# A scheduling planner whose costs for the time before the second mixture of experts become finer

## The chip, the cores and the metric

The kernel runs on one core of a Trainium2 chip. The metric is the device time of one execution in microseconds; the median of three runs before the change is 1993.34 us (1993.1 to 1995.27).

## The reference

Attention over 4 batches and 8 heads (576 tokens, head size 64) with a causal mask and a bias from a running sum, then a dense two-layer network with a gated activation, then a mixture of eight experts whose weights come out of eight rounds of row and column balancing:

```python
def _attn_ref(q, k, v, s):
    scores = np.matmul(q, k.transpose(0, 1, 3, 2)) / np.sqrt(D)
    cum = np.cumsum(np.maximum(s, 0.0), axis=-1)
    bias = -(cum[:, :, :, None] - cum[:, :, None, :])
    scores = np.where(causal, -1e9, scores + np.minimum(bias, 0.0))
    ...
    return np.matmul(attn, v)

def _moe_ref(x, w_in, w_out):          # 2304 x 512, hidden size 2048
    h = x @ w_in
    g = h * (1.0 / (1.0 + np.exp(-1.702 * h)))
    return g @ w_out

def _moe2_ref(x, w_gate, w1, w2):      # 8 experts, hidden size 1024
    P = balanced(np.exp(x @ w_gate))   # eight rounds
    for e in range(E):
        out += P[:, e:e + 1] * (np.maximum(x @ w1[e], 0.0) @ w2[e])
```

## The kernel before, in words

The program has three stages that overlap. **Attention** runs over 64 heads (each of the 32 is taken in two parts, 256 and 320 query rows). TensorE computes scores (`sp`), VectorE adds the mask and finds the extreme (`sm`, the ISA rows), ScalarE takes the exponential, TensorE turns the result (`tp`), it is copied to `pf` (early heads, one copy) or to `ph` and `pl` (later heads, two halves in 16 bits), TensorE multiplies by v (`op`), and VectorE finishes the head: a sum, a reciprocal, and the product `xg`. There is one bank for `op`, so the next head's `op` begins only when `xg` of the last is done. Finished rows are turned (`xtp`) into `xh` and `xl`.

**The first mixture** (in the code `moe`, it is one dense network) goes over nine blocks of 256 tokens and eight pairs of hidden slices. `hp` is the first product and `acc` the second; between them stand `t` (ScalarE's tanh, a VectorE product), `gh` (a cast) and `gl` (the rest). Its weights come as 64-bit words and have to be converted first: 32 chunks, each with two ScalarE passes over `st`, a VectorE operation `t<-st`, a cast to `wih` or `woh`, and a difference to `wil` or `wol`. Seven blocks are interleaved with attention; the last two run together, as `accw`, at its end. **The second mixture** (experts) follows; its operations are `A` to `D`, `h`, `y`.

What runs when is decided by a planner, the class `Sequencer`, while the program is built. Every operation is handed to `submit`, which asks `cost` for its duration; operations of TensorE are issued at once, those of the other engines are held and issued in the order in which the model says they can start (`run`, `issue`, `depend`). TensorE's next unit of work is chosen in the main loop: of six kinds (value products, turns, scores, first mixture last) the first whose inputs the model has ready at TensorE's modelled time. So the costs set the order of instructions on all engines, and nothing else about the program. They also set which engine takes a copy or a difference:

```python
    def any_copy(out, in_):
        if seq.load("DVE") <= seq.load("ACT"):
            nc.vector.tensor_copy(out, in_)
        else:
            nc.scalar.copy(out=out, in_=in_)

    def any_less(out, a, b, bias=POOL_BIAS):
        engine = nc.vector if seq.fine or seq.load("DVE") + bias <= seq.load("POOL") else nc.gpsimd
        engine.tensor_tensor(out=out, in0=a, in1=b, op=ALU.subtract)
```

The flag `fine` is set in `begin_second`, ahead of `accw`; from there on the finer costs were in use before the change too.

Of the kernel before, what the change touches and what calls it, by code (L numbers as in the profile page):

```python
# [10 lines left out]
F32R = mybir.dt.float32r  # L11
# [22 lines left out]
BYTES = {F32: 4, F32R: 4, I32: 4, F16: 2, BF16: 2, U8: 1}  # L34
# [4 lines left out]
N_KF = 4  # L39
ADDING = 3.6  # L40
AFTER_OWN = 34
N_F = 14
NEXT_V = 11
LATE = 3000.0
# [5 lines left out]


class Op:
    __slots__ = ("engine", "call", "cost", "ready", "end", "waits", "after", "rank", "number", "nbytes", "late", "tail")


class Sequencer:
# [10 lines left out]
    def __init__(self):  # L67
        self.free = dict.fromkeys(self.ENGINES, 0.0)
        self.held = {e: [] for e in self.ENGINES}
        self.touched = {}  # L70
        self.earlier = {}
        self.rings = {}
        self.dma = self.issued = 0.0
        self.rank = 0
        self.holding = False
        self.fine = False
        self.late = 0.0
        self.count = 0
        self.outside = set()
# [50 lines left out]
    def cost(self, engine, what, out, ins, sums=False):  # L130
        n = max(self.size(x) for x in [out] + ins[:2])
        psum = any(x.space == PSUM for x in ins)
        if self.fine:
            if engine == "PE":
                return self.size(out) * (4 if ins[0].dtype == F32 else 1) / 2.4 + (13 if ins[0].dtype == F32R else 2.7)
            by = any(self.size(x) == 1 for x in ins[1:]) and n > 1
            if engine == "DVE":
                quick = what in ("tensor_copy", "tensor_scalar") and not psum
                return 66 + 60 * by + n / (1.92 if quick else 0.96)
            if engine == "ACT":  # L140
                return (50 if psum else 90) + 100 * by + 93 * sums + n / 1.2
        if engine == "PE":
            n = self.size(out)
            if what == "transpose":
                return 2 * n / 2.4
            slow = ins[0].dtype == F32 or ins[0].dtype == F32R and n < 256
            return n * (4 if slow else 1) / 2.4
        if engine == "DVE":
            quick = what in ("tensor_copy", "tensor_scalar") and not psum
            return 70 + n / (1.92 if quick else 0.96)  # L150
        if engine == "ACT":
            return 90 + n / 1.2
        return 80 + n * {"memset": 0.3, "tensor_scalar": 2.7}.get(what, 2.24)


    def submit(self, engine, what, call, outs, ins, adds=False):
        op = Op()
        op.engine, op.call, op.end, op.rank, op.number = engine, call, None, self.rank, self.count
        op.ready, op.waits, op.after, op.nbytes, op.tail = 0.0, set(), [], 0, 0
        op.late = self.late + (2000 if self.fine and self.rank else 0)  # L160
        self.count += 1
        if what == "dma_start":
            op.cost = 60 if engine == "SP" else 1000
            op.nbytes = self.size(outs[0]) * outs[0].shape[0] * (2 if self.fine and outs[0].dtype == F16 else 4)
            if adds and self.fine:
                op.nbytes *= ADDING
        else:
            sums = len(outs) > 1
            op.cost = self.cost(engine, what, outs[0], ins, sums) + (190 if sums and not self.fine else 0)
            if self.fine:  # L170
                op.tail = {"DVE": 85, "ACT": 110}.get(engine, 0) + 90 * sums
        for ap, writes in [(x, False) for x in ins] + [(x, True) for x in outs]:
            name = ap.tensor.name
            if name in self.outside:
# [19 lines left out]
    def depend(self, op, on):  # L194
        if on.end is None:
            op.waits.add(on)
            on.after.append(op)
        elif self.fine and on.engine == op.engine != "PE" and not on.nbytes:
            op.ready = max(op.ready, on.end + AFTER_OWN)
        elif on.engine != "PE" or op.engine != "PE":  # L200
            op.ready = max(op.ready, on.end + LATENCY.get((on.engine, op.engine), LATENCY.get(on.engine, 0)))

    def issue(self, op):
        for x in sorted(op.waits, key=lambda x: x.number):
            if x.end is None:
                self.issue(x)
        e = op.engine
        start = max(self.free[e], op.ready)
        self.free[e] = start + op.cost
        op.end = start + op.cost + op.tail  # L210
        if op.nbytes:
            self.issued = max(self.issued, start) + 475
            self.dma = max(self.dma, self.issued + 1200) + op.nbytes / 360
            op.end = self.dma + 440 + op.late
        if op in self.held[e]:
            self.held[e].remove(op)
        op.call()
        op.call = None
        for x in op.after:
            x.waits.discard(op)  # L220
            self.depend(x, op)
        op.after = None

    def when(self, op):

# [2035 lines left out]
```

## Time and profile before

| | |
|---|---|
| median of three runs | 1993.34 us |
| the profiled execution | 1995.91 us |
| its span, first to last instruction | 1994.1 us |
| TensorE busy | 98% of the span |
| VectorE, ScalarE, GpSimd busy | 72%, 62%, 17% |
| first `hp`, first `accw` | 55.3 us, 573.67 us |

All instructions are recorded by one helper, so that they all carry its line, L279; they are told apart by the names of their tiles. The busy share of TensorE is high because its matmuls follow each other closely; gaps show in the view of who waits for whom. In that view and in the order of time, the bracket behind a row is the engine's idle time just before it and the instruction that ended it. "head 8" below is the eighth reciprocal over `stats` on VectorE.

### The profile page before, as it was taken

Reading aid. Unit: us, or ns where it says so; the run is one execution under the profiler, and the core shown is the slowest. Engines: PE = TensorE matmul, PEld = TensorE weight load, DVE = VectorE, ACT = ScalarE, POOL = GpSimd, SP = SyncE. Lnnn points to the kernel's source line nnn. Section 1 sums busy time; section 2 is a strip of 40 time slices with the busy share of each in tenths; the row PEclk is TensorE's granted clock in tenths of the full one; section 3 lists DMA queues with packets and bytes.
Section 4 is the critical chain, followed back from the end, with each engine's and each line's share of the span. In section 5 each row is a group of like instructions: output and inputs, shape, how many; then the busy total and the mean of one; then the engine's idle time right before and its main releaser. Section 6 shows DMA issues by size and latency. Waiting matters only on the chain.

```text
span 1994.1 us, 41095 instructions
## 1 busy us (share of the span) xinstructions
PE 1956.2 (98%) x15683; PEld 1575.5 (79%) x15683; DVE 1427.6 (72%) x3240; ACT 1227.5 (62%) x2525; POOL 335.0 (17%) x376
## 2 busy tenths in 40 slices
PE   6999999999999999999999999999999999999999
PEld 5889999999988677777777777777777777777777
DVE  5886776776743776887877767776787776776656
ACT  4776765766643665665666666656666666565343
POOL 3565444443300000000000011111100001111000
PEclk9999999999999999999999999999999999999999
DMA  7555444454335544565484565666648556566331
GB/s 221 159 178 181 138 131 138 129 146 116 86 94 186 208 152 146 202 232 182 147 273 133 153 186 156 172 197 184 167 120 261 147 150 186 156 172 183 119 130 43
DMA packets 230100, 322.11 MB, mean 162 GB/s; under 512 B 38272, under 2 KB 156224, under 8 KB 229904
## 3 DMA queue, kind: packets, MB, share of 16 engines
q1 hardware_dynamic: 216944, 295.90, 45.2%
q0 software_dynamic: 12960, 23.60, 8.2%
q8 instruction: 123, 2.02, 0.4%
q14 instruction: 73, 0.60, 0.1%
HBM read 230.85 MB, written 84.34 MB: 158 GB/s over the span
## 4 chain that ended last, share of the span: by engine, by line
PE 81%; DVE 9%; ACT 6%; DMA 2%; issue 1%; SPq 0%; POOL 0%; ACTq 0%; DVEq 0%
PE C L279 16%; PE A L279 16%; PE D L279 16%; PE hp L279 8%; PE B L279 8%; PE acc L279 5%; PE op L279 3%; PE sp L279 3%; PE tp L279 2%; ACT h L279 2%; PE accw L279 2%; DVE h L279 2%; DVE t L279 1%; DVE hst L279 1%; PE accx L279 1%
## 5 line engine op out<-in xcount | busy, mean ns | idle before, releaser
L279 PEld LDWEIGHTS <-h 128*128 128x128 f16 x6048 | 591.3, 98 | 86.3 <-issue 7.6
L279 PEld LDWEIGHTS <-w1o 128*128 128x128 f16 x4036 | 394.6, 98 | 255.1 <-issue 4.5
L279 POOL DMA_DIRECT2D acc_d<-y x90 | 77.8, 865 | 1186.5 <-DVE y L279 662.1
L279 PE MATMUL C<-xt,w1o 128*128 128x384 f16 x1152 | 218.6, 326 | 1.4 <-DVE hst L279 1.4
L279 PE MATMUL D<-xt,w1o 128*128 128x384 f16 x1152 | 218.4, 326 | 0.0
L279 PE MATMUL D<-w2o,h 128*128 128x256 f16 x1728 | 217.7, 273 | 0.2 <-ACT y L279 0.2
L279 PE MATMUL A<-xt,w1o 128*128 128x384 f16 x1152 | 214.8, 326 | 0.1
L279 PE MATMUL A<-w2o,h 128*128 128x256 f16 x1728 | 212.2, 273 | 1.7 <-ACT B L279 1.4
L279 PE MATMUL C<-w2o,h 128*128 128x256 f16 x1728 | 208.4, 273 | 2.5 <-DVE y L279 1.7
L279 DVE SCALAR_TENSOR_TENSOR h<-hst,h 128x768 f16<-128x768 f32 (+1 forms) x192 | 139.1, 755 | 55.9 <-ACT h L279 55.9
L279 ACT COPY C<-B 128x384 f32<-128x384 f32 (+1 forms) x168 | 71.5, 426 | 153.8 <-PE B L279 92.7
L279 PE MATMUL hp<-xh,wih 128*128 128x256 f32 (+1 forms) x512 | 154.4, 302 | 1.3 <-DVE t L279 0.7
L279 PE MATMUL hp<-xl,wih 128*128 128x256 f32 (+1 forms) x512 | 152.0, 297 | 0.0
L279 PE MATMUL hp<-xh,wil 128*128 128x256 f32 (+1 forms) x512 | 151.8, 297 | 0.0
L279 ACT ACTIVATE h<-hst 128x768 f16<-128x768 f32 (+1 forms) x192 | 126.2, 678 | 3.8 <-DVE hst L279 3.8
L279 ACT ACTIVATE sm<-sm,stats 64x576 f32<-64x576 f32 (+4 forms) x160 | 94.5, 600 | 34.0 <-DVE stats L279 33.7
L279 PE MATMUL acc<-gh,woh 128*128 128x256 f32 x384 | 110.9, 289 | 0.0
L279 PE MATMUL B<-w2o,h 128*128 128x256 f16 x864 | 110.5, 273 | 0.1
L279 PE MATMUL B<-xt,w1o 128*128 128x384 f16 x576 | 109.3, 326 | 0.0
L279 PE MATMUL acc<-gl,woh 128*128 128x256 f32 x384 | 108.5, 282 | 0.0
L279 PE MATMUL acc<-gh,wol 128*128 128x256 f32 x384 | 108.3, 282 | 0.0
L279 ACT COPY B<-A 128x384 f32<-128x384 f32 (+1 forms) x168 | 70.2, 425 | 58.4 <-PE A L279 57.6
(242 smaller groups left out, 4041.8 us busy)
## 6 DMA issues: line engine op xcount, KB each, us to landing
xt<-xc_d SPq DMA_DIRECT2D x168, 384.0 KB
wm<-in_moe_w_dram SPq DMA_DIRECT2D x112, 256.0 KB
w2o<-w_d SPq DMA_DIRECT2D x56, 512.0 KB
wr<-in_moe_w_dram SPq DMA_DIRECT2D x112, 256.0 KB
w_d<-wo SPq DMA_DIRECT2D x98, 256.0 KB
acc_d<-y POOLq DMA_DIRECT2D x90, 256.0 KB, 4.8
kq<-in_qk_dram SPq DMA_DIRECT2D x32, 448.0 KB
st<-in_moe_w_in_dram SPq DMA_DIRECT2D x16, 512.0 KB
```

The costliest lines, as they stand in the source:

```text
L279: self.seq.submit(self.name, what, lambda: method(*args, **named), outs, ins, "accum_op" in named)
```

## The change

The finer costs, until now used after `begin_second` only, are used from the start. For VectorE and ScalarE this means another base duration, 60 or 100 ns more where an operand is one number per row, no flat 190 ns for an operation with a second output, a tail of 85 or 110 ns (90 more with a second output) after which a result counts as there, and 34 ns between two operations of one engine. TensorE gets 2.7 or 13 ns per matmul, a weight load that shows where the matmul before it is shorter, and twice the time for everything until 6300 ns have passed without a gap of over 50 ns (`array`). No operation of the program is added or taken away but for the choice of engine.

```diff
--- before.py
+++ after.py
@@ -39,6 +39,7 @@
 N_KF = 4
 ADDING = 3.6
 AFTER_OWN = 34
+WARM = 6300
 N_F = 14
 NEXT_V = 11
 LATE = 3000.0
@@ -50,7 +51,7 @@
 
 
 class Op:
-    __slots__ = ("engine", "call", "cost", "ready", "end", "waits", "after", "rank", "number", "nbytes", "late", "tail")
+    __slots__ = ("engine", "call", "cost", "ready", "end", "waits", "after", "rank", "number", "nbytes", "late", "tail", "load")
 
 
 class Sequencer:
@@ -74,6 +75,7 @@
         self.rank = 0
         self.holding = False
         self.fine = False
+        self.cold, self.since, self.streamed = True, 0.0, 0.0
         self.late = 0.0
         self.count = 0
         self.outside = set()
@@ -133,30 +135,25 @@
         if self.fine:
             if engine == "PE":
                 return self.size(out) * (4 if ins[0].dtype == F32 else 1) / 2.4 + (13 if ins[0].dtype == F32R else 2.7)
-            by = any(self.size(x) == 1 for x in ins[1:]) and n > 1
-            if engine == "DVE":
-                quick = what in ("tensor_copy", "tensor_scalar") and not psum
-                return 66 + 60 * by + n / (1.92 if quick else 0.96)
-            if engine == "ACT":
-                return (50 if psum else 90) + 100 * by + 93 * sums + n / 1.2
         if engine == "PE":
             n = self.size(out)
             if what == "transpose":
-                return 2 * n / 2.4
+                return 2 * n / 2.4 + 3
             slow = ins[0].dtype == F32 or ins[0].dtype == F32R and n < 256
-            return n * (4 if slow else 1) / 2.4
+            return n * (4 if slow else 1) / 2.4 + (13 if ins[0].dtype == F32R else 2.7)
+        by = any(self.size(x) == 1 for x in ins[1:]) and n > 1
         if engine == "DVE":
             quick = what in ("tensor_copy", "tensor_scalar") and not psum
-            return 70 + n / (1.92 if quick else 0.96)
+            return 66 + 60 * by + n / (1.92 if quick else 0.96)
         if engine == "ACT":
-            return 90 + n / 1.2
+            return (50 if psum else 90) + 100 * by + 93 * sums + n / 1.2
         return 80 + n * {"memset": 0.3, "tensor_scalar": 2.7}.get(what, 2.24)
 
 
     def submit(self, engine, what, call, outs, ins, adds=False):
         op = Op()
         op.engine, op.call, op.end, op.rank, op.number = engine, call, None, self.rank, self.count
-        op.ready, op.waits, op.after, op.nbytes, op.tail = 0.0, set(), [], 0, 0
+        op.ready, op.waits, op.after, op.nbytes, op.tail, op.load = 0.0, set(), [], 0, 0, 0
         op.late = self.late + (2000 if self.fine and self.rank else 0)
         self.count += 1
         if what == "dma_start":
@@ -166,9 +163,10 @@
                 op.nbytes *= ADDING
         else:
             sums = len(outs) > 1
-            op.cost = self.cost(engine, what, outs[0], ins, sums) + (190 if sums and not self.fine else 0)
-            if self.fine:
-                op.tail = {"DVE": 85, "ACT": 110}.get(engine, 0) + 90 * sums
+            if engine == "PE":
+                op.load = 110 if BYTES[ins[0].dtype] == 4 else 27
+            op.cost = self.cost(engine, what, outs[0], ins, sums)
+            op.tail = {"DVE": 85, "ACT": 110}.get(engine, 0) + 90 * sums
         for ap, writes in [(x, False) for x in ins] + [(x, True) for x in outs]:
             name = ap.tensor.name
             if name in self.outside:
@@ -195,7 +193,7 @@
         if on.end is None:
             op.waits.add(on)
             on.after.append(op)
-        elif self.fine and on.engine == op.engine != "PE" and not on.nbytes:
+        elif on.engine == op.engine != "PE" and not on.nbytes:
             op.ready = max(op.ready, on.end + AFTER_OWN)
         elif on.engine != "PE" or op.engine != "PE":
             op.ready = max(op.ready, on.end + LATENCY.get((on.engine, op.engine), LATENCY.get(on.engine, 0)))
@@ -206,6 +204,8 @@
                 self.issue(x)
         e = op.engine
         start = max(self.free[e], op.ready)
+        if e == "PE" and not self.fine:
+            start = self.array(op, start)
         self.free[e] = start + op.cost
         op.end = start + op.cost + op.tail
         if op.nbytes:
@@ -220,6 +220,19 @@
             x.waits.discard(op)
             self.depend(x, op)
         op.after = None
+
+    def array(self, op, start):
+
+        idle = start > self.free["PE"] + 50
+        if idle:
+            self.since = start
+        if start - self.since > WARM:
+            self.cold = False
+        by = 2 if self.cold else 1
+        op.cost *= by
+        begin = start + max(0.0, by * op.load - (0.0 if idle else self.streamed))
+        self.streamed = op.cost
+        return begin
 
     def when(self, op):
 
```

From the first `accw` on, VectorE, ScalarE, GpSimd and TensorE have the same instructions in the same order as before; ahead of it, 19 operations more stand on VectorE, 22 fewer on ScalarE and 3 more on GpSimd. Two places in the order follow.

VectorE between the eighth and the ninth head, before. `sm` belongs to the ninth head's scores, `pf` to its turned results, `xl` to the first mixture's input, `st` and `t64` to the conversion of weights:

```order
L279 ISA sm_547,stats_124<-sp_562,mask_120,stats_124 64x288
L279 ISA stats_124 64x1
L279 ISA sm_569,stats_124<-sp_570,mask_120 128x384
L279 ISA stats_124 128x1
L279 COPY pf_579<-tp_574 128x512
L279 ISA sm_593,stats_124<-sp_594,mask_120 128x512
L279 ISA stats_124 128x1
L279 TENSOR_TENSOR xl_128<-xtp_582,xh_127 128x4x128
L279 CAST one0_112<-kq_360 128x896
L279 SCALAR_TENSOR_TENSOR t64_280<-st_258 128x512
L279 COPY pf_621<-tp_615 128x320
L279 TENSOR_TENSOR xl_128<-xtp_601,xh_127 128x4x128
```

The same place after the change, from the cast of the tenth head's keys (`one0`) on:

```order
L292 CAST one0_112<-kq_340 128x896
L292 ISA sm_561,stats_124<-sp_567,mask_120,stats_124 64x288
L292 ISA stats_124 64x1
L292 TENSOR_TENSOR xl_128<-xtp_546,xh_127 128x4x128
L292 CAST woh1_78<-t64_283 128x512
L292 SCALAR_TENSOR_TENSOR t64_349<-st_262 128x512
L292 COPY pf_589<-tp_585 128x384
L292 TENSOR_TENSOR xl_128<-xtp_553,xh_127 128x4x128
L292 ISA sm_593,stats_124<-sp_594,mask_120 128x384
L292 ISA stats_124 128x1
L292 TENSOR_TENSOR wol1_79<-t64_349,woh1_78 128x512
L292 COPY pf_614<-tp_609 128x512
```

The copy of the ninth head's first turned block, `pf_589`, now has a conversion `t64`, a cast `woh1` and an `xl` right ahead of it (another conversion, `t64_283`, stands just above the rows shown); before, that copy, `pf_560`, stood two rows above the rows shown. A difference, `wol1`, now stands ahead of the second copy `pf_614`.

TensorE while the fifth to eighth head end, before. `vtp` and `vbp` are two small matmuls for the scaling of v; the products `op` of the fifth head stand behind `vtp`:

```order
L279 MATMUL vtp_459<-ident_60,vmax_138 2x128
L279 MATMUL op_462<-vf0_133,pf_404 128x65 x2
L279 MATMUL op_462<-vf1_134,pf_404 128x65
L279 MATMUL tp_466<-ident_60,sm_378 128x128 x3
L279 MATMUL op_487<-vf0_133,pf_438 128x65 x2
L279 MATMUL op_487<-vf1_134,pf_438 128x65
L279 MATMUL vbp_491<-vd_412,ones_b_140 128x4
L279 MATMUL tp_493<-ident_60,sm_406 128x128 x3
L279 MATMUL op_515<-vf0_133,pf_470 128x65 x2
L279 MATMUL op_515<-vf1_134,pf_470 128x65
```

and after:

```order
L292 MATMUL op_455<-vf0_133,pf_404 128x65 x2
L292 MATMUL op_455<-vf1_134,pf_404 128x65
L292 MATMUL tp_460<-ident_60,sm_378 128x128 x3
L292 MATMUL vtp_472<-ident_60,vmax_138 2x128
L292 MATMUL op_482<-vf0_133,pf_439 128x65 x2
L292 MATMUL op_482<-vf1_134,pf_439 128x65
L292 MATMUL tp_488<-ident_60,sm_408 128x128 x3
L292 MATMUL vbp_503<-vd_414,ones_b_140 128x4
L292 MATMUL op_509<-vf0_133,pf_464 128x65 x2
L292 MATMUL op_509<-vf1_134,pf_464 128x65
```

`vtp` has moved from ahead of the fifth head's products to ahead of the sixth's; `vbp` has moved from behind the sixth head's products and ahead of a turn to behind that turn.

## Rows read from the trace of the kernel before

**Rows 1.** Busy time of TensorE over the span, from the page; us, share, instructions.

```profile
PE 1956.2 (98%) x15683; PEld 1575.5 (79%) x15683; DVE 1427.6 (72%) x3240; ACT 1227.5 (62%) x2525; POOL 335.0 (17%) x376
```

**Rows 2.** Stretches: us, then busy time of each engine (instructions), clock, DMA share, GB/s.

```profile
47.00:158.00 111.00, 103.78 (x913) 96.63 (x912) 97.13 (x254) 85.33 (x164) 65.84 (x63) 0.97 0.53 168
110.00:160.00 50.00, 44.81 (x392) 42.46 (x391) 47.47 (x109) 37.12 (x78) 34.05 (x31) 0.93 0.63 206
158.00:573.70 415.70, 411.17 (x4016) 393.76 (x4015) 293.22 (x863) 268.04 (x545) 174.53 (x191) 1.00 0.45 130
573.70:1994.00 1420.30, 1410.13 (x10643) 1059.67 (x10642) 1009.98 (x2034) 852.97 (x1776) 77.81 (x90) 1.00 0.56 168
```

**Rows 3.** The same view, two stretches in which the granted clock fell.

```profile
110.00:120.00 10.00, 7.49 (x56) 6.37 (x55) 9.59 (x28) 8.82 (x20) 5.53 (x6) 0.70 0.67 227
120.00:130.00 10.00, 10.00 (x95) 9.79 (x95) 8.97 (x20) 7.12 (x17) 6.69 (x8) 0.96 0.93 300
```

**Rows 4.** Who TensorE waited for, 8.6 to 573.6 us; total, times, longest.

```profile
PE op L279 <- DVE xg L279: 6.7, 7, 2.4
PE op L279 <- DVE pl L279: 2.6, 4, 1.1
PE vtp L279 <- DVE vmax L279: 1.8, 1, 1.8
PE op L279 <- DVE pf L279: 0.3, 1, 0.3
```

**Rows 5.** TensorE in order of time, opening; start, duration, idle before in brackets.

```profile
44.60 1.51 PE L279 MATMUL op<-vf,pf 128*128 128x65 f32 x6
48.15 1.05 PE L279 MATMUL tp<-ident,sm 128*128 128x128 f32 x4
50.64 0.60 PE L279 MATMUL xtp<-ident,xg 128*128 128x128 f32 x4
55.30 0.36 PE L279 MATMUL hp<-xh,wih 128*128 128x256 f32 x1
55.50 0.28 PE L279 MATMUL hp<-xl,wih 128*128 128x256 f32 x1
55.62 0.28 PE L279 MATMUL hp<-xh,wil 128*128 128x256 f32 x1
```

**Rows 6.** VectorE in order of time: reciprocals of the eighth, ninth and twenty-third head.

```profile
47.01 0.16 DVE L279 RECIPROCAL stats<-stats 128x2 f32<-128x2 f32 x1
55.24 0.17 DVE L279 RECIPROCAL stats<-stats 128x3 f32<-128x3 f32 x1
157.98 0.16 DVE L279 RECIPROCAL stats<-stats 128x2 f32<-128x2 f32 x1
```

**Rows 7.** VectorE groups by form, 47 to 170 us; busy, mean ns, idle before.

```profile
L279 DVE SCALAR_TENSOR_TENSOR t<-st 128x512 int32<-128x512 int32 x26 | 25.2, 974 | 1.1 <-POOL wol L279 0.7 <-ACT va L279 0.3
L279 DVE CAST woh<-t 128x512 fp32r<-128x512 f32 x10 | 7.0, 696 | 0.1
L279 DVE CAST wih<-t 128x512 fp32r<-128x512 f32 x8 | 6.2, 770 | 0.0
L279 DVE TENSOR_TENSOR wol<-t,woh 128x512 fp32r<-128x512 f32 x3 | 4.9, 1621 | 2.2 <-ACT woh L279 2.2
L279 DVE TENSOR_TENSOR one<-kq,one 64x320 fp32r<-64x320 f32 x3 | 4.3, 1420 | 0.1
L279 DVE TENSOR_TENSOR v<-va,v 128x128 f16<-128x128 f32 x4 | 4.0, 993 | 0.0
```

**Rows 8.** VectorE and GpSimd in order of time around 135 us.

```profile
135.19 1.80 DVE L279 SCALAR_TENSOR_TENSOR t<-st 128x512 int32<-128x512 int32 x1
135.14 1.29 POOL L279 TENSOR_TENSOR gl<-t,gh 128x512 fp32r<-128x512 f32 x1
```

**Rows 9.** The cast of gh on ScalarE (158 to 573.7 us) and on VectorE.

```profile
L279 ACT CAST gh<-t 128x512 fp32r<-128x512 f32 x43 | 26.6, 618 | 15.2 <-DVE t L279 14.3 <-DVE early L279 0.8
L279 DVE CAST gh<-t x7: 414/415/428, 133.6 to 451.5; 128x512 fp32r<-128x512 f32 x7
```

## The prediction

> **What bounds the kernel now.** I read the page first: TensorE is busy for 98% of the span [rows 1], so time can only come from its gaps, its order or its clock. Then the stretches: after the first `accw` at 573.7 us come 1420.3 us in which all four engines keep their order [rows 2], so nothing changes there and the whole change has to show ahead of 573.7 us. Then who TensorE waited for in that part: after the first transfer has landed there are fifteen groups of waits, 18.8 us in sum, the largest `op` for `xg` with 6.7 us, the smallest 0.3 us [rows 4]. Nearly all are waits for VectorE. The stretches say where: between 110 and 160 us VectorE works for 47.5 of 50 us, between 158 and 573.7 us for 293 of 416 [rows 2]. Early, while weights are converted, VectorE is the engine that is waited for; later TensorE paces itself. Last I read the opening in order of time. Four turns of one shape take 1.05 us at 48.15 and 0.60 us at 50.64 [rows 5]: until about 49 us TensorE works at the lower of its two levels, 1.2 GHz, then at 2.4. Later it falls once more: the granted clock is 0.70 and 0.96 in two stretches of 10 us from 110 us on [rows 3], 0.30 x 10 + 0.04 x 10 = 3.4 us of lost work, right where it waited for VectorE.
>
> **The change part by part.** It adds no work to TensorE. So I counted, in the two orders, what stands where, and priced it with durations of the trace.
>
> *Opening, up to the eighth head.* Before, `vtp` stands ahead of the fifth head's products and waits 1.8 us for `vmax` [rows 4]; now those products stand ahead of it. Two of the seven waits for `xg` get shorter by half of a conversion each (0.97 us, [rows 7]), together 1.0 us. The eighth head's products, at 44.60 us now [rows 5], come 2.8 us earlier, at 41.8. They take 1.5 us, and its reciprocal then follows with nothing but a sum ahead of it: 43.5 us, where it stands at 47.01 now [rows 6]. So the ninth head begins with a lead of 3.5 us.
>
> *Eighth to twenty-third head.* This lead is eaten by conversions. Between the eighth and the ninth reciprocal VectorE now has four `t<-st` where it had one, a cast to `woh` and a difference `wol`: 3 x 0.97 + 0.70 + 1.62 = 5.2 us more [rows 7]. That stretch takes 8.2 us now (47.01 to 55.24, [rows 6]). With 5.2 more, less the idle microsecond or so in it, the ninth head ends near 56.5, and the first `hp`, at 55.30 now [rows 5], comes near 57. Up to the twenty-third head VectorE has 3 `wol`, 3 casts to `wih`, 1 to `woh`, 2 conversions, 3 casts to `gh` and 1 `one` more and 4 `v` less: 4.86 + 2.31 + 0.70 + 1.95 + 1.24 + 1.42 - 3.97 = 8.5 us [rows 7, 9]; other kinds (copies to `pf`, scalings of v, scores) add 3.5, and 0.3 of it all lie ahead of the eighth head: 11.7 us. VectorE's 97.1 us of these 111 [rows 2] become 108.8. How long do they take? Without any gap 108.8 us, which ends at 43.5 + 108.8 = 152.3, or 5.7 us ahead of 158.0 [rows 6]; at the share of now (97.13 of 111.00, 0.875) 124.3 us, 9.8 us behind. At the 0.95 of the dense 50 us [rows 2] it would be 114.6 us and no difference. I take 0.93, nearer to the dense value because 8.3 of the 11.7 us lie ahead of the fifteenth head, where VectorE had idle time to give: 117.0 us, an end at 160.5, 2.5 us late. By then TensorE has done 420 matmuls of the first mixture instead of 408; 12 x 0.12 us (the step from 55.50 to 55.62, [rows 5]) = 1.4 us are in hand. Net **+1.1 us**, bounds -7.1 and +8.4.
>
> *Order on TensorE.* The first mixture's matmuls form 123 runs instead of 137. Its first matmul behind a turn takes 0.20 us to the next and 0.12 otherwise (55.30, 55.50, 55.62 in [rows 5]): at most 14 x 0.08 = 1.1 us. Not every run begins behind a turn, so I take half, **-0.6 us**, bounds -1.1 and 0.
>
> *Twenty-third head to the first `accw`.* I added up TensorE's work between two instructions that depend on each other through VectorE. Between a turn and the product that needs it, less than 2 us lie in 2 of 82 cases instead of none; between two heads' products, in 6 of 38 instead of 2. The planner sets consumers closer to producers. What such a case costs: `op` waited 0.96 us on average for `xg` (7 waits) and 0.65 us for `pl` (4 waits) [rows 4], so at most 4 x 0.96 + 2 x 0.65 = 5.1 us, and nothing if VectorE is free, as it is for 30% of that time [rows 2]. I take a quarter, **+1.2 us**. The eight more casts to `gh` on VectorE there (0.415 us, against 0.618 us on ScalarE, [rows 9]) cost nothing, since those idle 122 us hide 3.3 us; without that cover they would cost the 3.3.
>
> *Clock.* I keep the early end of the half clock and one later fall: **0**, bounds -3.4 (no fall) and +3.4 (two), from [rows 3].
>
> *Where the costs still miss.* At 135.19 us a `t<-st` takes 1.80 us, against a mean of 0.97 [rows 7, 8]; it began 0.05 us behind a GpSimd difference of 1.29 us and ended 0.56 us behind its end. Neither old nor new costs know of this. The Trainium skill, page "SBUF — State Buffer", section "Who interferes with whom", says that a VectorE operation with two inputs in SBUF, or in a two-port mode, and a GpSimd operation that reads SBUF lock each other out for a whole instruction. Against this change that rule speaks plainly: an estimate by it, a block of 1.29 us for each of the ten more conversions and differences, would make 12.9 us and a sum of some 2007 us; the trace agrees only for some, as the mean of 0.97 shows.
>
> The sum is 1.1 - 0.6 + 1.2 = +1.7 us: 1997.6 for an execution like the profiled one (1995.91), and **1995.0 us** against the median of 1993.34, which the profiled one exceeds by 2.6.
>
> **The rivals.**
>
> *The waits go* (faster). The new costs are nearer to the trace for a VectorE operation on scores and for ScalarE's copies, so TensorE may be given work that is ready. If half of the 18.8 us goes [rows 4] while the early stretch stays as above: -9.4 + 1.1, 1985.0 us. For it: most of these waits are single misjudgements. Against it: they sit where VectorE is full, and VectorE gets more.
>
> *VectorE does not fit* (slower). The extra work is stretched by the differences on GpSimd (1.80 us in [rows 8]), and its busy share stays at 0.875: +9.8 - 1.4 - 0.6 + 1.2 = +9.0, 2002.3 us. It decides at a share of 0.91: below it the loss passes 4 us. For it: 5.2 us of conversions stand ahead of the first `hp`, when TensorE has nothing else to do. Against it: VectorE had 13.9 idle us in that stretch [rows 2]. This is the mechanism on which the page's rule bears.
>
> *The clock stays low* (slower). `array` calls the array warm after 6300 ns without a gap; should the chip, with a gap of some 2.6 us in front of the ninth head's first products near 49 us, rise ten microseconds later than now, half of them is lost: 1995.0 + 5 = 2000 us. Against it: TensorE runs as densely ahead of that gap as before [rows 5].
>
> That the change moves nothing that can be measured is my forecast's own neighbourhood: 0.2%, 4 us, is about what a measurement of this kernel tells from no change.
>
> **How the numbers follow.** The forecast and its surroundings up to 4 us on either side of the median have 0.39, the waits that go 0.29, the full VectorE 0.24, the clock 0.08. So faster 0.29, same 0.39, slower 0.32. The predicted time is the likeliest case's, whose own range is 1990 to 1998. The bounds in sum would be -11.6 and +16.9; for eight times in ten I reach to just beyond the two large rivals: 1984 to 2005.
>
> **What would show it.** Right: the eighth reciprocal near 43.5, a gap of two or three microseconds in front of `op` for a copy `pf` near 50, the first `hp` near 57, the twenty-third reciprocal near 160.5 and the first `accw` near 575.4 us, with 1420 us behind it; VectorE busy for about 109 us between the eighth and the twenty-third head. Wrong: a first `accw` at 566 or earlier with less than half of the waits left (the first rival), or a VectorE share under 0.91 in that stretch (the second), or turns of 0.26 us still at 55 us (the third). A stretch behind `accw` that is longer or shorter by over 2 us would break the first step.

## The result and the profile after

The changed kernel takes **2020.14 us** (median of 4 runs, 2018.27 to 2023.99) against 1993.79 us in the same runs of before: a ratio of 1.0132, with an interval from 1.0119 to 1.0145. It is 26 us slower, outside the range that was given. The profiled execution has a span of 2017.8 us. Its page begins:

```profile
PE 1965.6 (97%) x15683; PEld 1578.9 (78%) x15683; DVE 1436.1 (71%) x3259; ACT 1218.2 (60%) x2503; POOL 337.8 (17%) x379
```

The view by stretches, in the columns of [rows 2], from the eighth to the twenty-third head, from there to the first `accw`, and behind it:

```profile
43.80:169.10 125.30, 112.36 (x939) 102.89 (x939) 108.06 (x276) 87.76 (x167) 76.05 (x72) 0.95 0.54 170
169.10:598.20 429.10, 414.68 (x3997) 392.52 (x3996) 292.77 (x871) 259.89 (x531) 168.72 (x189) 1.00 0.43 123
598.20:2017.80 1419.60, 1410.17 (x10644) 1059.76 (x10642) 1007.03 (x2023) 850.68 (x1768) 77.85 (x90) 1.00 0.56 168
```

Behind the first `accw` stand 1419.6 us where 1420.3 stood [rows 2]. The whole loss lies ahead of it, as the order said: the first `accw` begins at 598.21 instead of 573.51 us (the table of before has 573.67), 24.7 us later. In the profile it comes in two parts. The three reciprocals of [rows 6] are now here, VectorE in order of time:

```profile
43.81 0.17 DVE L292 RECIPROCAL stats<-stats 128x2 f32<-128x2 f32 x1
...
61.15 0.16 DVE L292 RECIPROCAL stats<-stats 128x3 f32<-128x3 f32 x1
...
169.09 0.17 DVE L292 RECIPROCAL stats<-stats 128x2 f32<-128x2 f32 x1
```

The eighth head comes 3.2 us earlier, the ninth 5.9 us later, the twenty-third 11.1 us later. By then TensorE has done 421 matmuls of the first mixture instead of 413, 8 x 0.12 = 1.0 us in hand. So **10.1 us** are lost up to the twenty-third head and the rest, **14.6 us**, between it and the first `accw`. Below, these two are called the loss *ahead of* and *behind* the twenty-third head, worked out in this way for every kernel.

The opening, TensorE in order of time, with the idle time before in brackets as in [rows 5]:

```profile
49.58 0.52 PE L292 MATMUL tp<-ident,sm 128*128 128x128 f32 x3 [1.74 <-DVE xl L292]
...
52.10 1.54 PE L292 MATMUL op<-vf,pf 128*128 128x65 f32 x6 [1.64 <-DVE pf L292]
...
61.48 0.41 PE L292 MATMUL hp<-xh,wih 128*128 128x256 f32 x1
```

The granted clock, third number from the end, in two stretches of the opening and in a later one:

```profile
48.20:51.60 3.40, 0.88 (x5) 0.58 (x5) 3.40 (x7) 1.25 (x2) 2.82 (x3) 1.00 0.49 144
51.60:61.90 10.30, 9.80 (x47) 8.78 (x48) 6.51 (x20) 5.95 (x11) 1.25 (x2) 0.50 0.33 109
157.40:160.80 3.40, 3.40 (x22) 3.31 (x23) 2.83 (x5) 2.21 (x5) 2.37 (x2) 0.51 0.73 226
```

The one fall ahead of the twenty-third head in the kernel before, of which [rows 3] show the two ends:

```profile
114.00:120.80 6.80, 5.91 (x39) 5.46 (x40) 6.29 (x16) 5.62 (x13) 4.24 (x6) 0.50 0.52 160
```

There are two waits for VectorE, 3.4 us in sum, one of them for the `pf` copy that the order showed behind conversions. In the 3.4 us around them TensorE is at its higher level and works for 0.88 us. Then follow 10.3 us at the lower level, 1.2 GHz, with 9.8 us of work: some 5.1 us of it are lost, and 1.7 us more from 157.4 us on. The kernel before loses 3.4 us in its one fall. So the clock makes 3.4 us of the 10.1, less some 0.5 us, since it first rises at 48.2 us here and at 49.1 before. (The view has a record of the clock only from that first rise on and says 1.00 ahead of it; the scores of 288 columns stand 0.24 us apart there, at 46.92, 47.16 and 47.40 us, which is 1.2 GHz.)

Who TensorE waited for up to the first `accw`, where [rows 4] had 6.7 us for `xg` and 18.8 in sum:

```profile
PE op L292 <- DVE xg L292: 9.4, 11, 2.0
...
PE hp L292 <- DVE t L292: 3.2, 3, 1.2
PE tp L292 <- ACT sm L292: 3.1, 5, 1.1
PE op L292 <- DVE xgl L292: 2.8, 4, 1.0
PE op L292 <- DVE pl L292: 2.5, 5, 0.8
```

All rows of this view from 160 us to the first `accw` add up to 13.9 us in 20 waits, against 4.5 us in 8 before. The view counts a wait only from the modelled end of the matmul ahead of it. Counted by the distance between two starts, beyond the distance that this pair of matmuls usually has (its 20th percentile in both kernels together), 39.3 us are lost there against 22.3, and 29.0 against 23.5 between 40 and 160 us, the clock's share included: 22.5 of the 24.7 us. The other 2.2 us I can't place.

### The profile page after: what moved, and what is told of

Read it like the earlier page. It is cut to its first block, busy times and chain, and to the rows that moved or that the text cites. A ratio compares the mean times of both kernels' runs of the same rounds, so it can differ in the third digit from the quotient of the medians.

```text
span 2017.8 us, 41085 instructions
## 1 busy us (share of the span) xinstructions
PE 1965.6 (97%) x15683; PEld 1578.9 (78%) x15683; DVE 1436.1 (71%) x3259; ACT 1218.2 (60%) x2503; POOL 337.8 (17%) x379
## 4 chain that ended last, share of the span: by engine, by line
PE 70%; DVE 7%; ACT 6%; DMA 1%; issue 1%; SPq 0%; POOL 0%; ACTq 0%; DVEq 0%; POOLq 0%
PE C L292 16%; PE A L292 16%; PE D L292 16%; PE B L292 8%; PE hp L292 5%; PE acc L292 3%; ACT h L292 2%; PE accw L292 2%; DVE h L292 2%; DVE hst L292 1%; PE op L292 1%; PE tp L292 1%; DVE sa L292 1%; PE sp L292 1%; DVE sb L292 1%
## 5 line engine op out<-in xcount | busy, mean ns | idle before, releaser
L292 DVE SCALAR_TENSOR_TENSOR t<-t,hp 128x512 f32<-128x512 f32 x72 | 49.1, 682 | 86.0 <-ACT t L292 83.5
```

Of the source, the lines that this page charges most:

```text
L292: self.seq.submit(self.name, what, lambda: method(*args, **named), outs, ins, "accum_op" in named)
```

## The experiments

The prediction had VectorE as the engine that is waited for, and a planner that places consumers closer to producers. It did not say why. First the change was taken apart. Diffs are against the changed kernel unless a sentence says before.

**Which costs do it.** TensorE's old costs with all else new (`e1_pe_old`):

```diff
-                return 2 * n / 2.4 + 3
+                return 2 * n / 2.4
...
-            return n * (4 if slow else 1) / 2.4 + (13 if ins[0].dtype == F32R else 2.7)
+            return n * (4 if slow else 1) / 2.4
...
-        if e == "PE" and not self.fine:
-            start = self.array(op, start)
```

> The changed kernel with TensorE's costs as they were (no 2.7 or 13 ns per matmul, no weight load, no cold start); VectorE's and ScalarE's are the new ones. Theory M (the old costs of TensorE were short by a tenth, so that the plan asked for its inputs earlier than the chip needed them, and the change took that margin away): most of the 26 us come back, 1993 to 2001 us, first accw at 574 to 582. Theory V (the new, lower costs of VectorE's score operations let the plan load VectorE with more than it can do): the loss stays, 2015 to 2023 us.

Measured: 2001.88 us, ratio to before 1.0038 (1.0023 to 1.0053). The same lines the other way round, added to the kernel before (`e2_pe_new`):

> The kernel before with TensorE's new costs alone (matmul, weight load, cold start); VectorE's and ScalarE's are the old ones. Theory M: most of the loss is here, 2010 to 2022 us. Theory V: as before, 1990 to 1998 us.

Measured: 2025.86 us, 1.0160 (1.0144 to 1.0176). Theory V falls. Both lie a little above the ranges given for theory M. Behind the twenty-third head the first loses -1.5 us and the second 27.4: TensorE's new costs make that part. Ahead of it they lose 9.4 and 6.9 us: there either half of the change is enough.

The cold start (`e3_no_cold`):

```diff
-        by = 2 if self.cold else 1
+        by = 1
```

> The changed kernel without the doubled time of the cold TensorE. Theory C (the opening's order alone, which the doubled time made, costs what stands up to the 23rd head, 11 us, and what follows from it): 2005 to 2010 us, and the ninth head's reciprocal back near 55 us from 61. Theories M and V: the opening may move by 5 us, the loss behind the 23rd head (13 us) stays, 2012 to 2022 us.

Measured: 2023.34 us, 1.0146 (1.0129 to 1.0163). Of this, 6.9 us are lost ahead of the twenty-third head and 20.5 behind it. The cold start isn't it. That leaves the 2.7 and 13 ns per matmul. A flat 10% on TensorE's costs in the kernel before, with nothing else (`e5_pe_flat_10`):

```diff
-                return 2 * n / 2.4
+                return 1.1 * 2 * n / 2.4
...
-            return n * (4 if slow else 1) / 2.4
+            return 1.1 * n * (4 if slow else 1) / 2.4
```

> The kernel before with every cost of TensorE ahead of the second mixture 10% higher and nothing else: no weight load, no cold start, no step per matmul. Theory R (what counts is how long TensorE's work is in the plan beside that of the other engines): 2010 to 2025 us. If weight load and cold start did it: 1990 to 1998 us.

Measured: 2011.87 us, 1.0087 (1.0068 to 1.0106), with -2.7 us ahead of the twenty-third head and +18.4 behind it. TensorE's price alone makes the loss behind. In the trace of before the step of one `hp` is 0.12 us [rows 5]; 256 / 2.4 = 107 ns is what the old plan reckoned, 120 ns the new one. So the right price is the harmful one.

**Is it luck?** The planner's order jumps with any cost, so the kernel before might only be a lucky draw. Three nudges that make nothing more right: 3 ns on the base costs of VectorE and ScalarE, in the kernel before and in the changed one (`e6_before_nudge_a`, `e8_after_nudge`), and 7 ns on a delay in the kernel before (`e7_before_nudge_b`):

```diff
-            return 70 + n / (1.92 if quick else 0.96)
+            return 73 + n / (1.92 if quick else 0.96)
...
-            return 90 + n / 1.2
+            return 93 + n / 1.2
```

> The kernel before with the base costs of VectorE and ScalarE 3 ns higher, 70 to 73 and 90 to 93. This makes no cost more right. Theory L (the order of before is a lucky one among many that the same rules can give, and any change of a cost loses it): 2000 to 2015 us. Theory R, which needs a change in the ratio of engines: 1989 to 1998 us.

> The kernel before with the delay behind a TensorE operation at 204 ns instead of 197, nothing else. Theory L: 2000 to 2015 us; theory R: 1989 to 1998 us.

> The changed kernel with the base costs of VectorE and ScalarE 3 ns higher, 66 to 69 and 50 or 90 to 53 or 93. Theory L: anywhere among other orders, 2000 to 2030 us, as likely below as above 2020. Theory R: 2013 to 2026 us.

Measured: 1997.68 us, 1.0012 (1.0003 to 1.0021); 1999.13 us, 1.0019 (1.0009 to 1.0028); 2028.22 us, 1.0162 (1.0146 to 1.0177). A nudge costs 2 to 8 us here. The third lies above the range given for theory R and inside the one for theory L. All the same, the two draws near the kernel before lie more than 20 us below every draw near the changed one (2020 to 2028 us, the third and fourth experiments included). Before is a good draw by some 3 us; the 26 us are not luck.

**What are the waits made of?** If inputs are merely asked for too late, a fixed margin helps (`e4_margin`):

```diff
-                t = max(t, x[3].end + 200)
+                t = max(t, x[3].end + (200 if self.fine else 700))
```

> The changed kernel, in which the choice of TensorE's next work ahead of the second mixture counts data as there 500 ns later (700 ns behind the end of the operation instead of 200). The costs and hence the planned times stay. Theory M, which says that inputs are asked for too late ahead of their use: the waits behind the 23rd head go, 2000 to 2010 us. Theory V: the margin does not help an engine that is full, 2016 to 2024 us.

Measured: 2021.75 us, 1.0138 (1.0123 to 1.0153). No help, with 9.5 us lost ahead of the twenty-third head and 16.8 behind it, though theory V was already out: theory M as I had put it falls too. So I had the planner print its own planned start of every operation, and compared it with the trace: how much later than planned an operation begins, less the same figure of TensorE at that moment. From 160 us to the first `accw` VectorE is on average 0.05 us *ahead* of the plan before the change and 0.50 us *behind* it after; over 1 us behind are 3% of its operations before and 19% after. In the changed kernel's plan TensorE has 0.3 us there in gaps of over 100 ns. The waits are not planned; VectorE and ScalarE fall behind the plan, and a fixed margin on TensorE's choices doesn't stop them from falling.

Two things could be the cause. One is that VectorE's operations without an operand in PSUM take longer than any cost says: those of 64 and more elements per row add up to 111 us in the new plan ahead of `accw` and to 166 us in its trace, less a tail of 80 ns each, 1.49 times. Those with an operand in PSUM add up to 207 us in both. ScalarE's work is 331 us in the plan and 326 in the trace (less 110 ns each), GpSimd's 229 and 262. The trace tells when VectorE is stretched: of these 314 operations the 171 that overlap with no GpSimd instruction take 59.9 us where the plan has 58.4, and the 143 that overlap with one take 106.0 us instead of 52.8. Those with an operand in PSUM take their planned time beside GpSimd as well, 112.8 and 112.8 us. In the kernel before, its plan has 51.9 us for the overlapping ones, and they take 106.9. This is read from the overlap; no run took GpSimd's work away.

The other is transfers. These are the rows of ScalarE's waits for transfers from 160 us to the first `accw`, in the kernel before:

```profile
ACT wb L279 <- DMA wa<-in_moe_w_dram: 9.4, 4, 4.4
ACT one L279 <- DMA kq<-in_qk_dram: 5.5, 8, 1.5
```

and in the changed one:

```profile
ACT one L292 <- DMA kq<-in_qk_dram: 21.7, 17, 3.4
...
ACT xb L292 <- DMA xc_d<-xb: 8.2, 6, 3.8
ACT wm L292 <- DMA wm<-in_moe_w_dram: 6.6, 4, 2.8
...
ACT wb L292 <- DMA wa<-in_moe_w_dram: 5.5, 5, 2.0
```

All such rows add up to 23.0 us in 24 waits before and 50.9 us in 43 after. But a transfer is not longer than the plan has it. The 43 of the changed kernel took, from issue to landing, the planned time on average (0.01 us less). What is late is their issue: from 160 us to the first `accw` SyncE issues transfers on average 0.90 us later than planned, counted as for VectorE above, and 0.27 us before the change. Which of the engines that SyncE waits for begins this is not shown.

ScalarE takes its instructions in order, so what stands behind the cast `one` is late too. One such case in the changed kernel, ScalarE, VectorE and TensorE in order of time:

```profile
295.89 0.62 ACT L292 CAST one<-kq 128x512 fp32r<-128x512 f32 x1 [1.45 <-DMA kq<-in_qk_dram]
296.41 0.80 ACT L292 ACTIVATE sm<-sm,stats 128x128 f32<-128x128 f32 x2
297.12 0.49 ACT L292 ACTIVATE wb<-wa,early 128x256 f16<-128x256 f32 x1
...
297.64 0.76 DVE L292 SCALAR_TENSOR_TENSOR wb<-wa,early,wb 128x256 f16<-128x256 f32 x1 [2.29 <-ACT wb L292]
298.44 0.42 DVE L292 TENSOR_TENSOR wa<-wa 128x256 f32<-128x256 f32 x1
...
298.95 0.51 ACT L292 ACTIVATE wb<-wa,early 128x256 f16<-128x256 f32 x1 [1.34 <-issue]
...
299.49 0.48 DVE L292 SCALAR_TENSOR_TENSOR wb<-wa,early,wb 128x256 f16<-128x256 f32 x1 [0.63 <-ACT wb L292]
...
300.35 0.35 DVE L292 SCALAR_TENSOR_TENSOR xg<-op,vpow,stats 128x128 f32<-128x128 f32 x1
...
300.75 0.22 PE L292 MATMUL op<-v,ph 128*128 128x65 f16 x2 [1.11 <-DVE xg L292]
```

The transfer of `kq` holds ScalarE, ScalarE's `wb` holds VectorE, VectorE's `wa` holds ScalarE's second `wb` (the profile names no releaser for it, but in the program it reads this `wa`), that one holds VectorE again, `xg` stands behind it, and TensorE waits for `xg`. The last row names VectorE; the chain begins with a transfer 5 us earlier.

**Does the ratio or the price count?** TensorE's costs at 0.9 (`e9_pe_90`), and everybody else's at 1.15 (`e11_others_115`):

```diff
             op.cost = self.cost(engine, what, outs[0], ins, sums)
+            if engine == "PE" and not self.fine:
+                op.cost *= 0.9
```

> The changed kernel with every cost of TensorE ahead of the second mixture multiplied by 0.9; weight load, cold start and all new costs of the other engines stay. Theory R, now with its mechanism (VectorE's real work is 57 us longer than its new costs, as it is stretched while GpSimd works; VectorE falls behind the plan and TensorE waits, unless the plan has TensorE fast as well, so that the real TensorE gives the time back at a steady rate): the stretch from the 23rd head to the first accw, 429 us in the changed kernel, falls to 408 to 420, the sum to 1998 to 2010, the rest being the opening's. If single misplaced units and not the rate did it: 2013 to 2026 us.

> The changed kernel with all costs of VectorE, ScalarE, GpSimd and SyncE ahead of the second mixture at 1.15 times, TensorE's as changed. Theory R: TensorE's work is then again shorter beside the others' in the plan, by as much as in the kernel before; 1996 to 2008 us, the stretch from the 23rd head to the first accw at 410 to 421. If TensorE's absolute price matters: 2014 to 2026 us.

Measured: 2007.24 us, 1.0062 (1.0047 to 1.0077), and 2013.34 us, 1.0092 (1.0077 to 1.0107). The first has 9.4 us left behind the twenty-third head, the second 16.2. The second is outside the 1996 to 2008 us of theory R. The ratio of the engines is not what counts: raising the others leaves the planned time of a transfer as it is, and ScalarE still waits 45.8 us for transfers.

The missing cost on VectorE and GpSimd (`e10_vector_full_price`), and every transfer counted as landed 1.5 us later (`e14_transfers_late`). Since a transfer takes its planned time, the second is a reserve and not a price:

```diff
             op.cost = self.cost(engine, what, outs[0], ins, sums)
+            if not self.fine and engine == "POOL":
+                op.cost *= 1.14
+            if not self.fine and engine == "DVE" and self.size(outs[0]) >= 64 and not any(x.space == PSUM for x in outs + ins):
+                op.cost *= 1.4
```

> The changed kernel with VectorE's operations of 64 and more elements per row that touch no PSUM at 1.4 times their cost and GpSimd's at 1.14, which is what they take on average in its trace. Theory R with the stretching by GpSimd as the missing cost: the lag goes, 2000 to 2012 us. If only TensorE's own price matters, or if costs that are right on average have no reserve: 2014 to 2026 us.

```diff
-            op.end = self.dma + 440 + op.late
+            op.end = self.dma + 440 + op.late + (0 if self.fine else 1500)
```

> The changed kernel in which the plan counts every transfer ahead of the second mixture as landed 1.5 us later. Theory T (ScalarE, which takes its instructions in order, stands behind the casts of kq that are placed at the planned landing; it waited 21.7 us for these behind 160 us, 5.5 us in the kernel before): its waits for kq fall to 5 to 10 us, 2005 to 2014 us. If only the stretching of VectorE by GpSimd makes the lag: 2015 to 2025 us.

Measured: 2014.42 us, 1.0098 (1.0082 to 1.0115), and 2009.46 us, 1.0076 (1.0061 to 1.0091). The first lies in the range of its rival, costs without a reserve, the second in that of theory T. They change different halves. The price on VectorE takes the loss ahead of the twenty-third head from 10.1 to 2.3 us and leaves 15.5 behind; its stretch from the eighth to the twenty-third head, which was 125.3 us long, is now:

```profile
44.70:157.80 113.10, 103.56 (x903) 96.35 (x902) 97.20 (x255) 88.66 (x172) 66.89 (x62) 0.97 0.53 167
```

VectorE's 108 us there are 97 again, as before: four copies `pf`, ten casts of weights and four differences fewer stand on it. Four conversions `t<-st` still stand between the eighth and the ninth head, as in the changed kernel, but the copies `pf` of the ninth head are on ScalarE, and the first `hp` comes at 52.23 us, ahead of the ninth head, where the changed kernel has it behind, at 61.48. The later transfers leave 10.3 us ahead and take the loss behind from 14.6 to 3.0 us; ScalarE's wait for `kq`, 21.7 us in the changed kernel, is

```profile
ACT one L292 <- DMA kq<-in_qk_dram: 1.3, 1, 1.3
```

Both together (`e15_all_full`, the two diffs above):

> Both at once: the changed kernel with VectorE's and GpSimd's full prices as in the tenth experiment and transfers 1.5 us later. If the lag comes from these two missing costs together: 1996 to 2006 us. If a plan that is right on average still needs a reserve for the spread, whatever its costs: 2008 to 2016 us.

Measured: **1992.36 us**, 0.9990 (0.9981 to 1.0000): the loss is gone, -1.2 us ahead and -1.1 behind. The opening is not the old one: the twenty-third head comes at 166.62 us, 8.6 us later than before, with 82 more matmuls of the first mixture done. Who TensorE waited for from 160 us to its first `accw`:

```profile
PE op L296 <- DVE pl L296: 0.9, 2, 0.5
PE hp L296 <- DVE t L296: 0.8, 1, 0.8
PE tp L296 <- ACT sm L296: 0.3, 1, 0.3
```

Two neighbours by the same rules, one with the 3 ns of the nudge above (`e17_all_full_nudge`), one with 1.3 and 1000 for 1.4 and 1500 (`e18_all_full_less`), ask whether that was a lucky order:

> The fifteenth experiment's kernel with the base costs of VectorE and ScalarE 3 ns higher, as in the eighth. If the missing costs made the gain, other orders by the same rules have it too: 1989 to 2002 us. If the fifteenth was a lucky order: 2004 to 2016 us.

> The fifteenth experiment's kernel with smaller surcharges: VectorE's operations without PSUM at 1.3 instead of 1.4 times, transfers 1.0 us later instead of 1.5. If the missing costs made the gain: 1990 to 2005 us, between the fifteenth and the changed kernel but nearer to the fifteenth. If it was a lucky order: 2004 to 2018 us.

Measured: 2004.03 us, 1.0047 (1.0030 to 1.0064), and 2003.40 us, 1.0044 (1.0029 to 1.0059). Both sides have a part in it. Behind the twenty-third head they lose -1.1 and +1.9 us, as the fifteenth; ahead of it 4.5 and 6.5, where the fifteenth had -1.2. Alone, the price and the reserve brought 5.7 and 10.7 us, which makes 2020.1 - 16.4 = 2003.7, just where the neighbours lie; of the 27.8 us of the fifteenth some 11 are a good draw, if the two simply add. Part of it is the clock: from 40 us to the twenty-third head the lower level costs 8.9 us in the fifteenth, in which the clock rises at 57.9 us (its `hp` stand 0.21 us apart until then) and does not fall again ahead of `accw`, 11.8 in the seventeenth and 13.7 in the eighteenth (8.0 before, 10.9 in the changed kernel).

**Is a reserve still worth something?** TensorE at 0.9 on top of both (`e16_all_full_pe_90`), and 5% less on TensorE in the kernel before (`e13_pe_flat_less_5`):

> The same with TensorE's costs multiplied by 0.9, so full prices for the others and a reserve by TensorE. Theory of the reserve: 1987 to 1998 us, the least of all waits behind 160 us (20 us or fewer). If the reserve does nothing once the others are priced: as the fifteenth experiment, within 4 us.

> The kernel before with every cost of TensorE ahead of the second mixture 5% lower, nothing else, so still further from the truth. If the theory of the reserve holds beyond the kernel before (the shorter TensorE's work in the plan, the less VectorE and ScalarE are behind it): waits behind 160 us at most as now, 1986 to 1995 us. If before is at the flat end of it, or the order is only a lucky one: 1995 to 2003 us.

Measured: 2002.62 us, 1.0041 (1.0026 to 1.0056), and 1993.74 us, 0.9992 (0.9982 to 1.0001). No: with VectorE's price and the reserve on transfers in, a short price of TensorE brings nothing. That kernel lies 10 us above the fifteenth, which neither expectation had, and where its neighbours lie. Still less on TensorE than before brings nothing either: its time is in the range given for the reserve only because the kernel before is in it too.

The rules of before up to the twenty-third head, then the new costs for VectorE and ScalarE with TensorE's old ones (`e12_before_then_new`, against before):

```diff
-            if self.fine:
+            if self.fine or self.exact:
...
+            seq.exact = n_fin >= 23
```

> The kernel before up to the end of the 23rd head; from then on the new costs of VectorE and ScalarE, with TensorE's old ones throughout. Theory R says the opening's loss comes from the new costs of VectorE and ScalarE there, and that these are harmless later while TensorE's are short: 23rd head at 158, first accw 568 to 574, 1988 to 1995 us. Rival: the stretch behind the 23rd head was faster in the first experiment only since more work lay ahead of that head; then 1995 to 2003 us.

Measured: 1998.36 us, 1.0019 (1.0010 to 1.0029). The new costs of these two engines cost 4.1 us behind the twenty-third head, within what a nudge does; the gain that I hoped for is not there, and the time lies in the rival's range.

The kernels side by side. *Late by plan* is the share of VectorE's operations from 160 us to the first `accw` that begin over 1 us later than the plan had it; *waits* are the sums over the instructions that begin between 160 us and the first `accw`:

| kernel | us | ahead of head 23 | behind | TensorE waits | ScalarE waits for transfers | late by plan |
|---|---|---|---|---|---|---|
| before | 1993.8 | 0 | 0 | 4.5 | 23.0 | 3% |
| changed | 2020.1 | 10.1 | 14.6 | 13.9 | 50.9 | 19% |
| e1 | 2001.9 | 9.4 | -1.5 | 4.1 | 17.4 | 5% |
| e2 | 2025.9 | 6.9 | 27.4 | 21.5 | 46.3 | 20% |
| e5 | 2011.9 | -2.7 | 18.4 | 15.4 | 32.0 | 16% |
| e10 | 2014.4 | 2.3 | 15.5 | 14.2 | 33.0 | 13% |
| e14 | 2009.5 | 10.3 | 3.0 | 8.0 | 7.3 | 9% |
| e15 | 1992.4 | -1.2 | -1.1 | 1.9 | 3.5 | 3% |
| e17 | 2004.0 | 4.5 | -1.1 | 1.4 | 4.9 | 3% |
| e18 | 2003.4 | 6.5 | 1.9 | 5.4 | 12.0 | 4% |

The two columns are not equally firm. *Behind*, the five kernels with later transfers (fourteenth to eighteenth) lose -1.1 to 4.7 us, the changed kernel and its kin without them (third, fourth, eighth, tenth, eleventh) 14.6 to 20.5. *Ahead*, the five with VectorE's price (tenth, fifteenth to eighteenth) lose -1.2 to 6.5 us, the changed kernel, the third, fourth, eighth and fourteenth 6.9 to 11.8, but the ninth 5.5 and the eleventh 2.7 without that price: the groups overlap.

No version beats both kernels by more than the measurement tells: the fifteenth stands 0.1% under before, with an interval that ends at 1.0000, and its neighbours are slower.

## Why the prediction was wrong

*Behind the first `accw`* nothing moves: right, 1419.6 against the 1420 that was given.

*Opening, up to the eighth head*: right. The reciprocal was to stand at 43.5 us and stands at 43.81.

*Eighth to twenty-third head*: the count of VectorE's work was right, its density wrong, and this step failed by 9.0 us: +1.1 was given, with bounds up to +8.4, and it is 10.1. 108.8 us were predicted and 108.06 measured, but I took a share of 0.93 and the stretch shows 108.06 / 125.30 = 0.86. That is near the value of the rival "VectorE does not fit" (0.875, a loss of 9.8 us less 1.4 for the matmuls in hand). That the number fits is partly luck, since some 3 us of the loss are the clock's. The error was to count the 8.3 us ahead of the fifteenth head as work that fits into idle time. 5.2 of them stand in front of the ninth head, where TensorE has nothing else. The wait for a `pf` copy came as forecast, 1.64 us at 52.10, but the ninth reciprocal came at 61.15, not near 56.5, the first `hp` at 61.48, not 57. The third rival came true in part with it: TensorE fell back to 1.2 GHz at 51.6 us, within the second of the two gaps, and rose at 61.9. In the tenth experiment, with these copies on ScalarE and one wait of 1.18 us in that place, the higher level begins at 48.5 us and stays until 123.6.

*Clock*: 0 was given, with 3.4 us as the bound above. It came to that bound: falls that cost 6.8 us against 3.4 before, less some 0.5 us for the earlier rise.

*Order on TensorE*: the 0.6 us of gain are not to be seen; 2.2 us of loss are not accounted for by waits or clock, and I didn't look for them further.

*Twenty-third head to the first `accw`*: this is the step that failed most, by 13.4 of the 23.0 us that the sum is off in the profile. I wrote +1.2 us with bounds 0 and 5.1, since a few consumers stood closer to their producers and VectorE was free for 30% of the time. It was 14.6. The closer consumers were the sign, but my price for one was a wait of before, in a plan that ran ahead of the chip. Before, the plan had TensorE 10% too fast. On the chip TensorE came later than planned to every input, and late transfers and operations that take long were there in time all the same; VectorE was 0.05 us ahead of its plan. With the right price this cover is gone, SyncE issues transfers 0.90 us behind the plan, and late transfers come through ScalarE's and VectorE's queues to TensorE. The first, second and fifth experiments show that TensorE's price makes this loss; the fourteenth to eighteenth show that counting transfers as landed 1.0 or 1.5 us later takes it away. That is a cover again, on the transfers in place of TensorE. The price of VectorE's stretched operations alone leaves 15.5 us of it.

*Where the costs still miss*: the rule that I weighed against the change (the Trainium skill, page "SBUF — State Buffer", section "Who interferes with whom") says that certain operations of VectorE and GpSimd in SBUF lock each other out. This trace agrees: only the operations in SBUF are stretched, 166 us instead of 111, and of these only the ones that overlap with a GpSimd instruction, 106.0 us instead of 52.8. The 12.9 us of that estimate were not the loss's form, since the stretching is hardly larger than before: VectorE's time beyond the 25th percentile of each kind of operation (same tiles, same shape) adds up to 54 us ahead of `accw` before and to 58 after. What may be new is what stood against it, which was not tried by itself: the plan before had 238 us for the operations with an operand in PSUM, which take 206, and this surplus of 32 us is gone with the old costs of the score operations.

The rival "the waits go" rested on the same mistake from the other side: better costs of some operations were to give TensorE work that is ready. They gave it work that the plan believed to be ready.

What stays open: single orders by the same rules differ by up to 12 us (the fifteenth and seventeenth experiments), mostly ahead of the twenty-third head, so that the 7.8 us which VectorE's price saved there in the tenth experiment are not beyond doubt, and a difference below some 10 us between two plans says little about the rule that made them.

## What to carry to other kernels

A model that sets an order can be good because its errors cancel: here a TensorE that was 10% too fast in the plan covered for transfers that are issued late, and perhaps a surplus of 32 us on VectorE's score operations for its stretched ones. Before making one cost right, compare the plan's start times with the trace engine by engine, the issue of transfers included. What falls behind is either priced too low, as VectorE's operations beside GpSimd, or held by others, as the transfers; there a reserve in the plan helped, though no transfer took longer than planned. When TensorE's waits name VectorE, follow the queue in front of the awaited instruction, through ScalarE to the transfer that held it.

## What was not expected of the hardware

TensorE kept its higher level for only 3.4 us (48.2 to 51.6) when it had worked for 0.88 us of them, and then took 10.3 us of almost full work at 1.2 GHz before it rose again; two waits of 3.4 us in sum went with 5.1 us lost to the clock. And VectorE's operations in SBUF took twice the plan's cost beside a GpSimd instruction and 1.03 times that cost without one, while those with an operand in PSUM took the plan's cost in both cases. The order hardly matters for it: VectorE's time beyond the 25th percentile is 47 to 63 us in the changed kernel, in the one before and in the ninth to eighteenth experiments.
